# Split attention tiles: scores from scaled float16 pieces of q and k instead of fp32r pieces

## The chip, the cores and the metric

The kernel runs on one NeuronCore of one Trainium2 chip. The metric is the device time of one execution in microseconds (us); three executions of the kernel before gave 1159.14, 1161.74 and 1163.35, median 1161.74. The profile is of one execution.

Engines: TensorE (PE, with its weight loads shown as PEld), VectorE (DVE), ScalarE (ACT), GpSimd (POOL) and the queue that issues the DMAs (SP).

## The reference

```python
def _attn_ref(q, k, v, tau):                     # q, k, v: (8, 8, 576, 64) float32
    scale = 1.0 / np.sqrt(q.shape[-1])
    scores = scale * np.matmul(q, k.transpose(0, 1, 3, 2))
    thresh = np.max(scores, axis=-1, keepdims=True) - tau
    scores = np.where(scores >= thresh, scores, -1000000000.0)
    scores = scores - np.max(scores, axis=-1, keepdims=True)
    attn = np.exp(scores)
    attn = attn / (np.sum(attn, axis=-1, keepdims=True) + 1e-09)
    return np.matmul(attn, v).astype(np.float32)

def _moe_ref(x, w_in, w_out, s, b):              # x: (4608, 512), d_ff 2048
    r = np.maximum(x @ w_in, 0.0)
    return ((s * (r * r) + b) @ w_out).astype(np.float32)
```

The attention output, with its heads side by side, is the x of the second function.

## The kernel before

Batch 0 is computed by 36 "plain" tiles in full fp32. Batches 1 to 7 are computed by visits: a visit is one pair of heads of one batch, 28 in all, and has nine split tiles of 128 queries (four of head A, four of head B, and one shared tile of the 64 queries that are left in each head), 252 in all. "Split" means that a float32 matrix is written as a high and a low piece, and a product is made from matmuls of pieces.

One split tile runs as follows (`split_tile`). PE makes 128x576 scores in one of two PSUM tiles, s or t (L525): four matmuls of 288 columns, or six for the shared tile. DVE takes the negated row maximum (L528, `top`). POOL makes the threshold from it (L530, `line`), ACT the exponential with `top` as its bias (L532), DVE applies the threshold and sums (L534), POOL and DVE make the divisor (L537, L539), ACT and DVE write the two float16 pieces of the weights (L540, L542, L543), and SP issues a DMA transpose of them into ea or eb (L548). With the transposed pieces PE makes the product with v (`with_v`, L558, 28 matmuls for a group of 256 or 320 queries).

Before its tiles, a visit is prepared. `Head.load` reads k and q of both heads twice, once into each half of the 128 partitions of rk and rq (four DMAs of 288 KB). `Head.prepare` makes, for each head, a high piece of k on ACT (L377) and a low piece on POOL (L378), scales q by 1/8 on POOL (L384), makes q's high piece on ACT (L387) and its low piece on POOL (L388), and the pieces of the 64 queries left over (L391, L392). All these pieces are fp32r, 4 bytes each. For the shared tile two SP copies per head (L381) move the pieces of k to the tiles ow6 and kt1. khi, klo and qs exist once for head A and once for head B. `Values.prepare` finds the largest |v| of the visit: a DVE maximum (L418), a matmul with ones that sums it over partitions (L420), three small DVE operations (L421, L423, L426), and a POOL operation that scales v (L429).

The FFN runs on blocks of 256 rows in 16 steps of f: `step` has 12 matmuls of 256 columns (L769, h), a relu, a square and a float16 copy on ACT (L773, L776, L777), a low piece on POOL (L778), and two groups of three matmuls of 512 columns (L784, o). There are 288 steps. They fill PE around the attention.

The order on each engine is static. Every operation is given to `Plan.add` with an engine, a cost (how long it occupies the engine, and when its result is there), the buffers that it reads and writes, and a wished time; `Plan.run` places all of them by a list schedule forward and backward, and emits them in order of planned start. Each engine executes its own list in that order and waits for the results that it needs.

```python
        SMALLEST, SPREAD, E_SPREAD = 2.0 ** -60, 2.0 ** 13, 2.0 ** 15
        pe((4, 6)[len(ti.heads) - 1], HS, scores, ti.kq(), [bk], i - SCORES_AHEAD)
```

## Time and profile before

| | |
|---|---|
| three executions | 1159.14, 1161.74, 1163.35 us |
| profiled execution, first to last instruction (span) | 1157.2 us |
| median less span | 4.5 us |
| PE busy | 1132.1 us, 98% of the span, 8844 matmul records |
| ACT busy | 930.5 us, 80% |
| DVE busy | 855.2 us, 74% |
| POOL busy | 780.9 us, 67% |
| DMA queue of SP | 162.9 MB, 70% of 16 engines' span |

The profile lists no time of its own for the profiled execution beside its span. Busy times are unions of intervals on an engine. Matmuls are pipelined and their ends are modelled, so PE's rows are best read by the distance from one start to the next. The DMA queue's own waits are not counted as busy.

### The profile page before, as it was taken

Reading aid. Unit: us, or ns where it says so; the run is one execution under the profiler, and the core shown is the slowest. Engines: PE = TensorE matmul, PEld = TensorE weight load, DVE = VectorE, ACT = ScalarE, POOL = GpSimd, SP = SyncE. Lnnn points to the kernel's source line nnn. Section 1 sums busy time; section 2 is a strip of 40 time slices with the busy share of each in tenths; the row PEclk is TensorE's granted clock in tenths of the full one; section 3 lists DMA queues with packets and bytes.
Section 4 is the critical chain, followed back from the end, with each engine's and each line's share of the span. In section 5 each row is a group of like instructions: output and inputs, shape, how many; then the busy total and the mean of one; then the engine's idle time right before and its main releaser. Section 6 shows DMA issues by size and latency. Waiting matters only on the chain.

```text
span 1157.2 us, 26174 instructions
## 1 busy us (share of the span) xinstructions
PE 1132.1 (98%) x8844; PEld 828.1 (72%) x8844; DVE 855.2 (74%) x1782; ACT 930.5 (80%) x2161; POOL 780.9 (67%) x1326
## 2 busy tenths in 40 slices
...
GB/s 265 343 140 22 47 142 165 178 188 181 155 177 169 165 165 164 170 162 154 164 148 164 133 137 166 170 131 180 159 165 128 160 158 176 119 20 1 20 19 19
DMA packets 361334, 164.52 MB, mean 142 GB/s; under 512 B 315120, under 2 KB 336112, under 8 KB 361200
## 3 DMA queue, kind: packets, MB, share of 16 engines
...
## 4 chain that ended last, share of the span: by engine, by line
PE 83%; DMA 5%; ACT 4%; DVE 3%; issue 2%; SPq 1%; POOL 1%; DVEq 0%; ACTq 0%; POOLq 0%
PE o L784 30%; PE h L769 30%; PE pv L558 8%; PE s L525 6%; PE t L525 6%; DMA eb<-en 2%; DMA ea<-in_q_dram 1%; ACT em L475 1%; PE pv L504 1%; DMA rk<-in_k_dram 1%; DMA iw<-in_moe_w_in_dram 1%; PE s L468 1%; PE h L698 1%; PE t L491 1%; DMA rq<-in_q_dram 1%
## 5 line engine op out<-in xcount | busy, mean ns | idle before, releaser
L769 PE MATMUL h<-xp,iw 128*128 128x256 f16 x3456 | 426.9, 273 | 3.5 <-ACT iw L773 3.4
L769 PEld LDWEIGHTS <-iw 128*128 128x128 f16 x3456 | 330.2, 98 | 87.7 <-issue 9.2
L784 PE MATMUL o<-ow,gh 128*128 128x512 f16 x1080 | 324.2, 382 | 0.7 <-DVE iw L798 0.7
L778 POOL TENSOR_TENSOR gl<-iw,gh 128x256 f16<-128x256 f32 x272 | 202.6, 746 | 118.1 <-ACT gh L777 95.7
L543 DVE SCALAR_TENSOR_TENSOR en<-em,st,en 128x576 f16<-128x576 f32 x252 | 241.4, 962 | 21.3 <-ACT en L540 20.6
L540 ACT ACTIVATE en<-em,st 128x576 f16<-128x576 f32 x252 | 192.8, 770 | 16.5 <-DVE st L539 13.5
L784 PE MATMUL o<-ow,gl 128*128 128x512 f16 x540 | 205.4, 380 | 0.0
L773 ACT ACTIVATE iw<-h 128x256 f32<-128x256 f32 x288 | 109.3, 380 | 111.4 <-PE h L769 100.7
L784 PEld LDWEIGHTS <-gh 128*128 128x128 f16 x1152 | 101.7, 99 | 76.6 <-issue 5.0
L530 POOL TENSOR_SCALAR st<-st,bound 128x1 f32<-128x1 f32 x252 | 108.7, 432 | 52.8 <-DVE st L528 25.9
L776 ACT ACTIVATE iw<-iw 128x256 f32<-128x256 f32 x288 | 119.5, 415 | 3.9
L777 ACT CAST gh<-iw 128x256 f16<-128x256 f32 x288 | 115.8, 402 | 5.4 <-PE o L784 1.6
L534 DVE SCALAR_TENSOR_TENSOR em<-t,st,em 128x576 f32<-128x576 f32 x126 | 102.3, 812 | 24.1 <-ACT em L532 13.5
L537 POOL TENSOR_SCALAR st<-st 128x1 f32<-128x1 f32 x252 | 79.2, 314 | 58.0 <-DVE em L534 30.1
L534 DVE SCALAR_TENSOR_TENSOR em<-s,st,em 128x576 f32<-128x576 f32 x126 | 102.2, 811 | 21.4 <-POOL st L530 10.0
L528 DVE TENSOR_REDUCE st<-t 128x1 f32<-128x576 f32 x126 | 94.7, 751 | 26.4 <-PE t L525 25.4
L532 ACT ACTIVATE em<-s,st 128x576 f32<-128x576 f32 x126 | 92.7, 736 | 23.9 <-DVE st L528 23.1
L528 DVE TENSOR_REDUCE st<-s 128x1 f32<-128x576 f32 x126 | 94.6, 751 | 21.3 <-PE s L525 18.6
L558 PE MATMUL pv<-eb,v 128*64 128x256 f16 (+1 forms) x784 | 106.4, 288 | 2.8 <-DMA eb<-en 2.1
L558 PE MATMUL pv<-ea,v 128*64 128x256 f16 (+1 forms) x784 | 107.5, 288 | 0.0
L532 ACT ACTIVATE em<-t,st 128x576 f32<-128x576 f32 x126 | 92.6, 735 | 16.7 <-DVE st L528 15.8
L784 PEld LDWEIGHTS <-gl 128*128 128x128 f16 x576 | 56.5, 98 | 68.8 <-POOL gl L778 1.1
(190 smaller groups left out, 1873.8 us busy)
## 6 DMA issues: line engine op xcount, KB each, us to landing
...
ow<-k SPq DMA_DIRECT2D x56, 216.0 KB, 3.0
...
kt<-k SPq DMA_DIRECT2D x56, 72.0 KB, 2.8
```

The lines of the kernel that those rows point to most:

```text
L525: nc.tensor.matmul(ps[:, hf], stat, kk(hf), start=(n == 0), stop=(n == len(seq) - 1))
L528: dve((667, 750), lambda: nc.vector.tensor_reduce(out=top, in_=ps, axis=mybir.AxisListType.XY, op=ALU.max, negate=True), [bk], [(ks_, 0)], ...
L532: act((636, 740), lambda: nc.scalar.activation(out=halves, in_=ps, func=AF.Exp, bias=top, scale=1.0), [bk, (ks_, 0)], [em_k], i - 0.5)
L534: dve((740, 900), lambda: nc.vector.scalar_tensor_tensor(out=halves, in0=ps, scalar=line, in1=halves, op0=ALU.is_ge, op1=ALU.mult, accum_o ...
L540: act((668, 774), lambda: nc.scalar.activation(out=pieces[:, 0:S], in_=ex, func=AF.Copy, scale=unit), [em_k, (ks_, 3)], [en_k], i)
L543: dve2((740, 825), lambda: nc.vector.scalar_tensor_tensor(out=pieces[:, S + T:2 * S + T], in0=ex, scalar=unit, in1=pieces[:, 0:S], op0=ALU ...
L558: nc.tensor.matmul(ps[j * D:(j + 1) * D], hd.v[:, (n + 1) % 5, u * D:(u + 1) * D], lazy[("ea", "eb")[j]][:, n, g.c0:g.c0 + g.n], start=(i ...
L769: nc.tensor.matmul(ps, wi[w][f][:, c * P:(c + 1) * P], x[:, u, c, :], start=(c == 0 and i == 0), stop=(c == NC - 1 and i == 2))
L776: act((320, 417), lambda: nc.scalar.activation(out=g(), in_=g(), func=AF.Square), [kg], [kg], at)
L777: act((308, 405), lambda: nc.scalar.copy(out=hi, in_=g()), [kg], [f"gh{k3}"], at)
L778: do((712, 735) if not self.last else (340, 425), lambda: eng.tensor_tensor(out=lo, in0=g(), in1=hi, op=ALU.subtract), [kg, f"gh{k3}"], [f ...
L784: nc.tensor.matmul(bank["o"][:, t, :], a[:, ts_], w, start=(f == 0 and i == 0), stop=(f == NF - 1 and i == 2))
```

## The change

For the 28 visits (`class Visit` takes the place of `Values` and of the loads and preparations of `Head`):

- k and q are loaded once, two heads on 128 partitions, two DMAs of 288 KB per visit, into rk[:, n] and rq[:, n] with n the visit's number modulo 2.
- Maxima of |k|, |q| and |v| are taken (three DVE reductions), summed over partitions by one bf16 matmul, and turned into powers of two. POOL scales k and q by them (the factor of q holds the 1/8), ACT makes their high pieces in float16 and POOL their low pieces, on both heads at once. The pieces are kept for two visits.
- For each head, SP copies stack the pieces: both 64-partition halves of `y` get the two pieces of k (2 copies of 64x1152 float16), the upper half the high piece of q and the lower half the low one (2 copies of 64x512). That is 8 copies per visit in place of 4. The four stacks live in the tiles ow6 to ow9; the weights that stood there move into the first half of iw6 to iw9.
- A tile's scores are the same number of matmuls of the same columns, from float16 operands. The shared tile uses the pieces themselves and a small tile qt16.
- Scores are now larger by a power of two. POOL's threshold takes a per-visit limit (wz column 2), ACT makes the bias by a 128x1 operation of its own (L557 of the changed kernel), and the exponential takes the scale from wz column 1.
- The matmuls that sum norms over partitions take bf16 ones and bf16 squares instead of fp32. The planner's price for a matmul becomes 0.417 ns a column plus 3 ns.

```diff
-    qt, kt1 = const("qt", [P, 2, P], F32R), const("kt1", [P, HS], F32R)
+    qt = const("qt", [P, 2, P], F32R)
...
-    vm = const("vm", [P, 2], F32R)
+    vm = [const(f"vm{i}", [P, 4], BF16) for i in range(2)]
...
-            lazy["k"] = sb("k", [P, 4, S], F32R)
+            lazy["k"] = sb("k", [P, 8, S], F16)
...
-        def q(j):
-            lazy["qs", j] = sb(f"qs{j}", [P, M], F32R)
-        for j in range(2):
-            claim([f"q{j}"], lambda j=j: q(j))
-        def kp():
-            lazy["kp"] = sb(f"ow{PAIRS_IN}", [P, 2 * DM], F32R)
-        claim(["kp", (f"w{PAIRS_IN}", "o")] + [("kp", j, c) for j in range(2) for c in (0, S + HS)], kp)
-        claim(["k", "khi0", "klo0", "khi1", "klo1"], k)
+        claim(["k"] + [("piece", n, c) for n in range(2) for c in range(4)], k)
+        for n in range(2):
+            for j in range(2):
+                def y(n=n, j=j):
+                    lazy["y", n, j] = sb(f"ow{STACKS_IN + 2 * n + j}", [P, 4 * DM], F16)
+                claim([f"y{n}{j}", (f"w{STACKS_IN + 2 * n + j}", "o")] + [("y", n, j, c) for c in range(4)], y)
...
-        plan.add("PE", (n * (0.44 * cols + 6.5), n * (0.44 * cols + 6.5) + 170), fn, r, w, at)
+        plan.add("PE", (n * (0.417 * cols + 3), n * (0.417 * cols + 3) + 170), fn, r, w, at)
...
+            self.n, self.wz, self.kwz = i % 2, wz[i % 3], f"wz{i % 3}"
+            self.kpc = [("piece", self.n, c) for c in range(4)]
+            self.kqt = [(f"qt16_{self.n}", j) for j in range(2)]
+
+        def piece(self, c):
+
+            return lazy["k"][:, 4 * self.n + c]
+
+        def keys_of(self, j, u):
+
+            return lazy["y", self.n, j][:, u * S:(u + 1) * S]
+
+        def queries_of(self, j):
+
+            return lazy["y", self.n, j][:, 2 * S:2 * S + M]
...
+            for key, buf, ap in ("rk", rk, kT), ("rq", rq, qT):
+                load(288, lambda buf=buf, ap=ap: nc.sync.dma_start(out=buf[:, n], in_=ap[bi, h2].rearrange("h d s -> (h d) s")),
+                     [], [(key, n)], at)
...
+            raw = [(rk[:, n], ("rk", n)), (rq[:, n], ("rq", n))]
             flat = rv.rearrange("p h t d -> p (h t d)")
-            top = bank["pv"][:, 510:512]
-            dve((730, 819), lambda: nc.vector.tensor_reduce(
-                out=vm[:, 0:1], in_=flat, axis=mybir.AxisListType.X, op=ALU.max, apply_absolute_value=True), kr, ["vm"], at)
-            pe(1, 64, lambda: nc.tensor.matmul(top, ones, vm, start=True, stop=True), ["vm", "ones"], ["pv"], at)
+            ks = []
+            for c, (t, keys) in enumerate([(t, [k]) for t, k in raw] + [(flat, kr)]):
+                w = t.shape[-1]
+                ks.append((f"vm{n}", c))
+                dve((67 + 1.04 * w, 150 + 1.04 * w), lambda c=c, t=t: nc.vector.tensor_reduce(
+                    out=vm[n][:, c:c + 1], in_=t, axis=mybir.AxisListType.X, op=ALU.max, apply_absolute_value=True),
+                    keys, [ks[-1]], at)
+            top = bank["pv"][:, 500 + 4 * n:504 + 4 * n]
+            ktop = ("top", 500 + 4 * n)
+            pe(1, 64, lambda: nc.tensor.matmul(top, onesb, vm[n], start=True, stop=True), ks + ["onesb"], [ktop], at)
             dve((72, 155), lambda: nc.vector.tensor_scalar(
-                out=x[:, 0:1], in0=top[:, 0:1], scalar1=SMALLEST, scalar2=None, op0=ALU.max), ["pv"], [kx], at)
+                out=x[:, 0:3], in0=top[:, 0:3], scalar1=SMALLEST, scalar2=None, op0=ALU.max), [ktop], [kx], at)
             dve((72, 155), lambda: nc.vector.tensor_scalar(
-                out=x.bitcast(I32)[:, 1:2], in0=x.bitcast(I32)[:, 0:1], scalar1=EXPONENT, scalar2=EXPONENT,
+                out=x.bitcast(I32)[:, 3:6], in0=x.bitcast(I32)[:, 0:3], scalar1=EXPONENT, scalar2=EXPONENT,
                 op0=ALU.bitwise_and, op1=ALU.bitwise_xor), [kx], [(kx, 1)], at)
             dve((72, 155), lambda: nc.vector.tensor_scalar(
-                out=x.bitcast(I32)[:, 2:3], in0=x.bitcast(I32)[:, 0:1], scalar1=EXPONENT, scalar2=None,
+                out=x.bitcast(I32)[:, 6:9], in0=x.bitcast(I32)[:, 0:3], scalar1=EXPONENT, scalar2=None,
                 op0=ALU.bitwise_and), [kx], [(kx, 2)], at)
+            pool((270, 192), lambda: nc.gpsimd.tensor_tensor(
+                out=x[:, 9:12], in0=x[:, 3:6], in1=spread[:, 0:3], op=ALU.mult), [(kx, 1), "spread"], [(kx, 3)], at)
+
+            for c, (t, key) in enumerate(raw):
+                up = x[:, 9 + c:10 + c]
+                pool((722, 742), lambda t=t, up=up: nc.gpsimd.tensor_scalar(
+                    out=t, in0=t, scalar1=up, scalar2=1.0, op0=ALU.mult, op1=ALU.mult), [key, (kx, 3)], [key], at)
+                act((612, 717), lambda c=c, t=t: nc.scalar.copy(out=self.piece(2 * c), in_=t), [key], [self.kpc[2 * c]], at)
+                pool((1385, 1420), lambda c=c, t=t: nc.gpsimd.tensor_tensor(
+                    out=self.piece(2 * c + 1), in0=t, in1=self.piece(2 * c), op=ALU.subtract),
+                    [key, self.kpc[2 * c]], [self.kpc[2 * c + 1]], at)
+            for j in range(2):
+                own = slice(j * D, (j + 1) * D)
+                for u in range(2):
+                    to = slice(u * D, (u + 1) * D)
+                    dma(144, lambda j=j, own=own, to=to: nc.sync.dma_start(
+                        out=lazy["y", n, j][to, 0:2 * S].rearrange("p (u s) -> p u s", u=2), in_=lazy["k"][own, 4 * n:4 * n + 2]),
+                        self.kpc[0:2], [("y", n, j, u)], at)
+            for j in range(2):
+                own = slice(j * D, (j + 1) * D)
+                for u in range(2):
+                    to = slice(u * D, (u + 1) * D)
+                    dma(64, lambda j=j, own=own, to=to, u=u: nc.sync.dma_start(
+                        out=self.queries_of(j)[to], in_=self.piece(2 + u)[own, 0:M]), [self.kpc[2 + u]], [("y", n, j, 2 + u)], at)
+                pool((330, 330), lambda j=j, own=own: nc.gpsimd.tensor_copy(
+                    out=qt16[n][own, :, j * T:(j + 1) * T], in_=lazy["k"][own, 4 * n + 2:4 * n + 4, M:S]),
+                    self.kpc[2:4] + ["qt16"], [self.kqt[j]], at)
+            pool((270, 192), lambda: nc.gpsimd.tensor_scalar(
+                out=self.wz[:, 1:2], in0=x[:, 6:7], scalar1=0.25 / SPREAD ** 2, scalar2=x[:, 7:8], op0=ALU.mult, op1=ALU.mult),
+                [(kx, 2)], [(self.kwz, 1)], at)
+            pool((270, 192), lambda: nc.gpsimd.tensor_scalar(
+                out=self.wz[:, 2:3], in0=x[:, 3:4], scalar1=spread[:, 3:4], scalar2=x[:, 4:5], op0=ALU.mult, op1=ALU.mult),
+                [(kx, 1), "spread"], [(self.kwz, 2)], at)
...
-                seq = ti.st()
+                c, j = slice(hf * HS, (hf + 1) * HS), ti.slot
+                if j is None:
+                    seq = [(qt16[va.n][:, u], va.piece(w)[:, c]) for u, w in ((0, 0), (0, 1), (1, 0))]
+                else:
+                    seq = [(va.queries_of(j)[:, ti.n * P:(ti.n + 1) * P], va.keys_of(j, w)[:, c]) for w in range(2)]
                 for n, (stat, kk) in enumerate(seq):
-                    nc.tensor.matmul(ps[:, hf], stat, kk(hf), start=(n == 0), stop=(n == len(seq) - 1))
-        pe((4, 6)[len(ti.heads) - 1], HS, scores, ti.kq(), [bk], i - SCORES_AHEAD)
+                    nc.tensor.matmul(ps[:, hf], stat, kk, start=(n == 0), stop=(n == len(seq) - 1))
+        pe(6 if ti.slot is None else 4, HS, scores, va.kpc[0:2] + va.kqt if ti.slot is None else [("y", va.n, ti.slot, c) for c in range(4)],
+           [bk], i - SCORES_AHEAD)
 
         dve((667, 750), lambda: nc.vector.tensor_reduce(
             out=top, in_=ps, axis=mybir.AxisListType.XY, op=ALU.max, negate=True), [bk], [(ks_, 0)], i - SCORES_AHEAD)
         pool((260, 263), lambda: nc.gpsimd.tensor_scalar(
-            out=line, in0=top, scalar1=-1.0, scalar2=line_, op0=ALU.mult, op1=ALU.add), [(ks_, 0), "bound"], [(ks_, 1)], i - 0.5)
-        act((636, 740), lambda: nc.scalar.activation(out=halves, in_=ps, func=AF.Exp, bias=top, scale=1.0),
-            [bk, (ks_, 0)], [em_k], i - 0.5)
+            out=line, in0=top, scalar1=-1.0, scalar2=va.wz[:, 2:3], op0=ALU.mult, op1=ALU.add), [(ks_, 0), (va.kwz, 2)], [(ks_, 1)], i - 0.5)
+        act((100, 200), lambda: nc.scalar.activation(out=bias, in_=top, func=AF.Copy, scale=va.wz[:, 1:2]),
+            [(ks_, 0), (va.kwz, 1)], [(ks_, 4)], i - 0.5)
+        act((636, 740), lambda: nc.scalar.activation(out=halves, in_=ps, func=AF.Exp, bias=bias, scale=va.wz[:, 1:2]),
+            [bk, (ks_, 4), (va.kwz, 1)], [em_k], i - 0.5)
...
-        pe(1, 64, lambda: nc.tensor.matmul(bank["pv"][:, col:col + m], ones.bitcast(F32), nm[:, 0:m], start=True, stop=True),
-           ["ones", knm] + [(knm, u) for u in range(n)], [ktop], at)
+        pe(1, 64, lambda: nc.tensor.matmul(bank["pv"][:, col:col + m], onesb, nm[:, 0:m], start=True, stop=True),
+           ["onesb", knm] + [(knm, u) for u in range(n)], [ktop], at)
```

Three places in the order of instructions show it.

GpSimd, middle of the program, before: the preparation of one pair of heads stands one step at a time between the small operations of tiles (L530, L537) and the FFN (L778).

```order
L388 TENSOR_TENSOR qs_1047<-rq,qs_1047 64x512
L530 TENSOR_SCALAR st_74<-st_74,bound 128x1
L778 TENSOR_TENSOR gl_109<-iw_223,gh_106 128x256
L378 TENSOR_TENSOR k<-rk,k 128x576
L537 TENSOR_SCALAR st_74<-st_74 128x1
L530 TENSOR_SCALAR st_75<-st_75,bound 128x1
L388 TENSOR_TENSOR qs_1048<-rq,qs_1048 64x512
```

GpSimd, middle of the program, of the change: L415 makes the visit's factors, L420 scales k and q, L423 makes the low pieces; L555 and L564 are the tiles' small operations, L807 the FFN's.

```order
L415 TENSOR_TENSOR vs_104<-vs_104,spread 128x3
L420 TENSOR_SCALAR rk<-rk,vs_104 128x576
L420 TENSOR_SCALAR rq<-rq,vs_104 128x576
L423 TENSOR_TENSOR k<-rk,k 128x576
L423 TENSOR_TENSOR k<-rq,k 128x576
L555 TENSOR_SCALAR st_70<-st_70,wz_91 128x1
L442 TENSOR_SCALAR wz_92<-vs_104 128x1
```

The four long operations of a visit moved together, behind one small operation that needs the sum made by PE.

ScalarE, middle of the program, before: an exponential (L532) waits for DVE alone.

```order
L532 ACTIVATE em_80<-t,st_71 128x576 [waits DVE_49]
L773 ACTIVATE iw_443<-h 128x256 [waits PE_49]
L391 CAST qt<-rq 64x64
L776 ACTIVATE iw_443<-iw_443 128x256 [waits Activation_49]
L777 CAST gh_108<-iw_443 128x256 [waits Activation_49]
```

ScalarE, middle of the program, of the change: L557 is the small operation for the bias, L559 the exponential.

```order
L557 ACTIVATE st_72<-st_72,wz_90 128x1 [waits DVE_49]
L559 ACTIVATE em_78<-t,st_72,wz_90 128x576 [waits PE_49,Activation_49]
L567 ACTIVATE en_77<-em_80,st_71 128x576 [waits DMAHW5_49,DVE_49]
L569 COPY en_77<-en_77 128x64 [waits Activation_49]
L557 ACTIVATE st_73<-st_73,wz_90 128x1 [waits DVE_49]
```

The wait for DVE moved to the small operation, and the exponential waits for it.

TensorE, of the change, between the sum of maxima of the fifth of the 28 visits and that visit's first scores: L406 is the matmul that sums the maxima, L813 the FFN's, L585 products with v, L708 a sum of norms, L549 scores (each row repeated as often as the prediction says).

```order
L406 MATMUL pv<-vm_82,onesb 128x4
...
L813 MATMUL o<-ow_891,gh_115 128x512
...
L549 MATMUL t<-ow_1548 128x288
...
L585 MATMUL pv<-ea,v_106 64x256
...
L708 MATMUL pv<-nsq_86,onesb 128x2
...
L549 MATMUL s<-ow_1397 128x288
```

Before, the matmul that sums the maximum of v (L420) stood behind the first scores of its visit in all 28 visits; now it stands ahead of them, and the scores need what follows from it.

## Rows read from the trace of the kernel before

**Rows 1.** Busy time by stretch: us, then us (instructions) of each engine, clock, DMA share, GB/s

```profile
40.00:135.00 95.00, 89.41 (x794) 68.61 (x793) 86.66 (x172) 88.67 (x172) 69.38 (x112) 1.00 0.41 126
135.00:270.00 135.00, 126.75 (x967) 91.00 (x966) 118.72 (x254) 113.64 (x264) 103.23 (x171) 0.97 0.83 162
270.00:1030.00 760.00, 756.34 (x5986) 555.80 (x5984) 608.48 (x1269) 638.79 (x1522) 566.13 (x958) 1.00 0.82 154
1030.00:1157.00 127.00, 121.85 (x831) 80.95 (x828) 14.05 (x26) 56.31 (x139) 21.34 (x34) 1.00 0.06 18
```

**Rows 2.** Longest waits of PE, 135 to 270 us: total, times, longest

```profile
PE s L525 <- DVE em L534: 5.7, 3, 3.1
```

**Rows 3.** Timeline of PE, 500 to 512 us: start, duration, what, how many

```profile
503.19 1.47 PE L769 MATMUL h<-xp,iw 128*128 128x256 f16 x12
504.50 0.59 PE L784 MATMUL o<-ow,gh 128*128 128x512 f16 x2
...
507.09 1.47 PE L769 MATMUL h<-xp,iw 128*128 128x256 f16 x12
508.32 0.77 PE L525 MATMUL t<-k,qs 128*128 128x288 f32 x4
508.94 0.61 PE L784 MATMUL o<-ow,gh 128*128 128x512 f16 x2
```

**Rows 4.** Groups of matmuls by form: count, busy us, mean ns, idle before

```profile
L525 PE MATMUL s<-k,qs 128*128 128x288 f32 x448 | 92.6, 328 | 5.9 <-DVE em L534 5.7
...
L525 PE MATMUL s<-ow,qt 128*128 128x288 f32 x70 | 15.2, 322 | 0.0
...
L525 PE MATMUL s<-kt,qt 128*128 128x288 f32 x14 | 4.1, 294 | 0.0
...
L679 PE MATMUL pv<-norm,ones 128*128 128x2 f32 x32 | 4.6, 214 | 0.2 <-ACT en L540 0.2
```

**Rows 5.** Chain that ended last, 200 to 210 us: start, us, what

```profile
204.65 2.02 PE pv L558 x28
```

**Rows 6.** Timeline, 671.4 to 673.2 us: a sum of maxima and what follows

```profile
671.61 0.25 PE L420 MATMUL pv<-vm,ones 128*128 128x2 f32 x1
...
672.37 1.82 POOL L429 TENSOR_SCALAR rv<-rv,vs 128x640 f32<-128x640 f32 x1 [0.22 <-DVE vs L426]
```

**Rows 7.** Timeline, 835.4 to 838.6 us: the same in another visit

```profile
835.50 0.35 PE L420 MATMUL pv<-vm,ones 128*128 128x2 f32 x1
...
838.26 0.79 POOL L429 TENSOR_SCALAR rv<-rv,vs 128x640 f32<-128x640 f32 x1
```

**Rows 8.** Groups of GpSimd by form

```profile
L378 POOL TENSOR_TENSOR k<-rk,k 128x576 fp32r<-128x576 f32 x56 | 83.0, 1483 | 9.0 <-ACT k L377 3.3 <-DMA ea<-en 2.8 <-PE pv L420 1.2
...
L388 POOL TENSOR_TENSOR qs<-rq,qs 64x512 fp32r<-64x512 f32 x56 | 74.1, 1323 | 4.8 <-ACT en L542 0.3
L384 POOL TENSOR_SCALAR rq<-rq,bound 128x576 f32<-128x576 f32 x56 | 46.7, 836 | 28.5 <-DMA rq<-in_q_dram 24.5 <-PE pv L420 2.1 <-issue 0.3
...
L432 POOL TENSOR_SCALAR vs<-vs 128x1 f32<-128x1 f32 x28 | 8.8, 316 | 2.4
```

**Rows 9.** DMA issues: count, KB each, median us from issue to landing

```profile
ow<-k SPq DMA_DIRECT2D x56, 216.0 KB, 3.0
...
kt<-k SPq DMA_DIRECT2D x56, 72.0 KB, 2.8
```

**Rows 10.** Groups of ScalarE by form

```profile
L542 ACT COPY en<-en 128x64 f16<-128x64 f16 x252 | 59.4, 239 | 0.8
L377 ACT CAST k<-rk 128x576 fp32r<-128x576 f32 x56 | 37.3, 666 | 7.2 <-PE t L525 4.5 <-PE h L769 1.0 <-issue 0.8
L387 ACT CAST qs<-rq 128x512 fp32r<-128x512 f32 x56 | 34.7, 619 | 2.2 <-POOL rq L384 1.6 <-PE s L525 0.3 <-issue 0.2
```

**Rows 11.** Group of VectorE by form

```profile
L528 DVE TENSOR_REDUCE st<-s 128x1 f32<-128x576 f32 x126 | 94.6, 751 | 21.3 <-PE s L525 18.6 <-PE pv L420 1.3
```

**Rows 12.** Timeline of PE, 128 to 136 us: the first scores of a split tile

```profile
135.05 0.77 PE L525 MATMUL s<-k,qs 128*128 128x288 f32 x4
```

129 lines of the change are left out of this document (50 added, 79 removed).

## The prediction

> **What bounds the kernel now.** I read busy time by stretch first. From 270 to 1030 us PE is busy 756.3 of 760 us at full clock, while ACT is busy 84% (638.8), DVE 80% and POOL 74% [rows 1]. So there PE's own work sets the time, and the other engines have 120 to 190 us to spare. From 135 to 270 us, the first visits, PE lacks 8.3 us and the clock's mean is 0.97, which is about 4 us more at full clock; the longest waits there are scores that wait for a PSUM tile [rows 1, 2]. The end, 1030 to 1157 us, is FFN alone: 648 of its first matmuls stand behind the last scores, before and after, so the change does not touch it. From 40 to 135 us ACT is busy 88.7 of 95 us, DVE 86.7 and PE 89.4: there no engine has much to spare.
>
> So I price the change by what it takes from PE's own work, and by the waits that it adds to PE.
>
> **The scores themselves.** The price of one fp32r matmul of 288 columns comes from starts on PE's timeline. Twelve h matmuls take 504.50 - 503.19 = 1.31 us, 109 ns each; twelve o matmuls 507.09 - 504.50 = 2.59 us, 216 ns each. Twelve h and four scores take 508.94 - 507.09 = 1.85 us, so four scores take 0.54 us, 135 ns each [rows 3]. In float16 I put 288 columns on the line through 256 columns (109) and 512 (216): 122.5 ns. There are 448 + 70 + 14 score matmuls on s [rows 4] and, by the order, as many on t: 1064. The saving is 12.5 ns x 1064 = 13 us; since starts are given to 10 ns, four scores lie between 0.52 and 0.56 us, and the saving between 8 and 19 us. I take 12.
>
> **Sums over partitions.** The 18 sums of norms are fp32, seen as two records each; all of them together are busy 4.6 us [rows 4]. As one bf16 pass they lose about half: -2 us, between 0 and -4.6. The sum of maxima stays one short matmul per visit.
>
> **The other engines.** POOL loses 56 subtractions of 1.48, 56 of 1.32 and 56 scalings of 0.84 us (203.8 us together) and gets 56 subtractions and 56 scalings of the first and last kind (129.7) and 84 small operations of 0.32 (26.5) [rows 8]: 48 us less; the short operations on the 64 queries left over stay about as many. DVE gets 56 more maxima over 576 columns, 0.75 us each [rows 11]: +42 us, which in the long stretch brings it from 80% to about 85%. ACT loses 56 casts of 0.67 and 56 of 0.62 us (72 us), gets 56 of 0.67 back (37), and 252 bias operations that the trace has no row for. The nearest is the 128x64 copy, 0.24 us [rows 10]; with one column it can't cost more, nor less than nothing: 0 to 60 us. ACT changes by -35 to +25 us over the 895 us of the split phase, and stays below 90%. None of the three becomes the bound. In a tile's own chain the bias operation adds at most 0.24 us between the maximum and the exponential; a score tile is held in one of two PSUM tiles while PE does nearly 7 us of other work (760 us for about 220 tiles is 3.4 us a tile), so that is covered. The copies move 832 KB a visit instead of 576, but the loads 576 instead of 1152: SP issues two DMAs more per visit and carries less.
>
> **The wait that the change adds.** This is the term that decides. Before, k's and q's pieces needed no sum, and the sum of v's maximum stood behind a visit's first scores. Now the sum stands ahead of them, and from it to the first scores runs one chain: three small DVE operations, POOL's factors, two scalings and two subtractions, and the copy of q's low piece by SP. Its price:
> - from the sum to POOL's first operation 0.76 us in a clean case [rows 6] and 2.76 us where DVE was taken [rows 7]; I take the middle, 1.8;
> - on POOL 0.32 + 2 x 0.84 + 2 x 1.48 = 4.96 us [rows 8]; by the order 0 to 5 other operations stand between, 0.6 us of them on the mean: 5.5 (5.0 to 6.6);
> - the copy, 2.8 us from issue to landing for 72 KB and 3.0 for 216 KB [rows 9], so 2.8 for 64 KB;
> - two hand-overs, POOL to SP and DMA to PE, for which I put 0.4 together, a choice.
>
> That is 10.5 us, with 8.5 and 12.3 as bounds. What covers it is the PE work that the order places between the sum and the first scores. Counted with 109, 216 and 122.5 ns for the three forms, and 2.02 us for 28 products with v [rows 5], it is 5.2 us at the fifth visit (12 o, 4 scores, 28 products), 7.8 at the third, 9.0 at the first, 9.6 to 15 elsewhere, and 11.2 in the middle. Where the cover is short, PE waits for the rest. At 10.5 us the 28 visits lack 13.1 us together, 9.5 of it in the first five; at 8.5 us they lack 4.0, at 12.3 us 39.5 (16.3 in the first five).
>
> A rule of the Trainium skill speaks to the copy's price: "DMA: Bandwidth & Descriptors", Anatomy of one DMA, fits a fixed 2.0 us and 436 GB/s, for GpSimd's path. By it a 64 KB copy would take 2.2 us, the chain 9.9, the lack 8.5 us and the time about 5 us less than mine. The trace agrees that size hardly matters (72 and 216 KB differ by 0.2 us), but not on the fixed part, and I keep the measured 2.8.
>
> The first five visits lie in the stretch where the kernel before already loses 8.3 + 4 = 12.3 us. Their loads and buffers are loosened: k and q come in two DMAs and every piece has two visits' room, so I take the old loss as replaced, by 9.5 us of new waits and some 2 us of clock: net -1. The later visits add 3.6 us.
>
> **The start.** Up to the first split scores (135.05 us before [rows 12]) PE's lists are nearly the same: 108 h, all 72 plain scores, 175 against 180 transposes, 36 against 30 o. But the first relu of the FFN is the 180th row of ACT instead of the 156th. ACT's mean from 40 to 135 us is 88.67 / 172 = 0.52 us an instruction [rows 1], so 24 rows are 12 us; most of it is plain tiles that PE also does earlier, with 25 more transposes and 30 more products ahead of the first h. I take +2.5 us, between 0 and +6.
>
> **The sum.** 1157.2 - 12 - 2 - 1 + 3.6 + 2.5 = 1148.3 us of span. The median of the runs is 4.5 us above the profiled span; with the same distance the forecast is **1153 us**, 0.8% faster.
>
> **Rivals.**
> - *The visits run free* (chance 0.20). The order lets sums, pieces and copies run early, and the chain keeps within its cover. For it: POOL loses 48 us, each buffer has two copies, and this kernel's old chain through POOL rarely held PE after 270 us. Against it: the cover in the order is what the planner thought just enough, and it counts a 64 KB copy at 1.8 us, not 2.8. Then the early loss of 12.3 goes but for some 2 us, and 1157.2 - 12 - 2 - 10 + 0 = 1133, or 1138 us with the 4.5. The shorter copy of the page named above points this way.
> - *Nothing is left over* (0.17). The float16 scores gain only the lower 8 us, the sums of norms nothing, and the start costs the full 6: 1157.2 - 8 - 1 + 3.6 + 6 = 1157.8, or 1162 us.
> - *The chain is longer than its cover in most visits* (0.18, slower). Place: first scores of each visit, PE waiting for the copies into y. At 12.3 us the first five lack 16.3 + 2 against 12.3, the others 23.2: 1157.2 - 14 + 6 + 23.2 + 2.5 = 1175, or 1179 us. It decides from a chain of about 11.2 us on, where the lack eats the 14 us that PE saves. For it: the chain has nine steps on four in-order engines, and DVE and POOL are the two that were late in [rows 7]; a long wait can also halve the clock for a while, as happened twice before 270 us. Against it: the planner's list puts the five POOL steps close together.
>
> That fp32r weight loads set the pace of the scores, so that float16 would save far more, is excluded: a matmul with its load takes 135 ns in all [rows 3], 12 to 13 ns above the float16 line.
>
> **Chances and range.** Forecast 0.45 (1147 to 1158 us), the rivals as given. I count 0.3% (3.5 us) as what a measurement of this kernel can tell from no change. Nearly all of the forecast and all of the first rival are faster by more: 0.63. The second rival and the edges of its neighbours are within: 0.19. The third is slower: 0.18. For 8 in 10 the range leaves out the far half of the free case (below 1142) and of the slow one (above 1168).
>
> **What would show it.** In the profile after, a tile's four score matmuls take 0.49 us from start to start instead of 0.54; the sums of norms are single records; PE from 270 to 1030 us still has under 10 us of idle time. PE's waits ahead of the score line name a DMA into ow6 to ow9 (or POOL), some 13 us in total, the longest at the third and fifth visits. ACT's bias operations take 0.1 to 0.24 us. The first split scores begin at 135 to 141 us. The prediction is wrong if these waits exceed 25 us or the clock falls again and again, or if PE's waits move to the products with v because the eight copies hold back SP's transposes; and, on the other side, if the first visits run without waits.

## The result, and the profile after

The changed kernel takes 1172.04 us (median of four executions, 1171.52 to 1179.10) where the kernel before took 1160.44 on the same chip: a ratio of 1.0121, 95% interval 1.0088 to 1.0154. It is 1.2% slower. The forecast was 0.8% faster, and the time lies above the forecast's range. The profiled execution took 1172.21 us with a span of 1170.4. The experiments ran on several chips; each ratio is to the kernel before on the same chip, where its median lay between 1159.0 and 1160.4. One execution of the experiment e13, the profiled one, took 1451.68 us at a mean granted clock of 0.75; its ratio leaves it out, and no time is read from its profile.

The first view is busy time by stretch, with the columns of [rows 1]; the last four lines are extra stretches around 270 us.

```profile
40.00:135.00 95.00, 81.92 (x750) 63.01 (x747) 84.33 (x177) 87.22 (x165) 52.09 (x91) 0.98 0.42 141
135.00:270.00 135.00, 116.99 (x895) 78.32 (x893) 115.11 (x240) 112.21 (x268) 93.73 (x176) 0.96 0.72 144
270.00:1030.00 760.00, 747.29 (x5998) 519.64 (x5997) 630.10 (x1320) 673.12 (x1657) 525.13 (x982) 1.00 0.74 147
...
257.00:271.00 14.00, 6.00 (x37) 3.62 (x33) 11.40 (x22) 7.65 (x15) 9.21 (x20) 0.62 0.78 149
271.00:285.00 14.00, 14.00 (x112) 9.96 (x111) 12.32 (x25) 11.83 (x30) 5.47 (x11) 0.89 0.58 145
...
264.00:268.00 4.00, 2.02 (x8) 0.98 (x7) 3.08 (x4) 3.56 (x7) 2.24 (x8) 0.50 0.85 166
...
276.00:280.00 4.00, 4.00 (x32) 2.88 (x30) 3.60 (x7) 3.13 (x10) 1.83 (x6) 1.00 0.75 163
```

Against [rows 1], PE is busy 7.5 us less from 40 to 135 us, 9.8 less from 135 to 270 and 9.1 less after that. From 257 to 271 us it works only 6 of 14 us. While it stands there, the granted clock falls to half (1.2 GHz); within the next 14 us it is back at 2.4 GHz. PE's longest waits from 100 to 290 us (total, times, longest):

```profile
PE pv L708 <- DVE nsq L764: 5.0, 1, 5.0
PE h L798 <- ACT iw L802: 4.7, 5, 1.9
PE s L549 <- DMA ow<-k: 3.6, 3, 2.4
PE h L798 <- DVE xp L782: 2.3, 1, 2.3
```

The groups by form, to be held against [rows 4] and [rows 10], show that the operations themselves came out much as forecast on PE, and longer on ACT. The first line is of the kernel before, the others of the changed one:

```profile
L532 ACT ACTIVATE em<-s,st 128x576 f32<-128x576 f32 x126 | 92.7, 736 | 23.9 <-DVE st L528 23.1
...
L559 ACT ACTIVATE em<-s,st,wz 128x576 f32<-128x576 f32 x126 | 104.0, 825 | 1.2
...
L549 PE MATMUL s<-ow 128*128 128x288 f16 x448 | 74.3, 289 | 4.2 <-DMA ow<-k 4.0 <-DVE em L561 0.2
L549 PE MATMUL t<-ow 128*128 128x288 f16 x448 | 73.8, 288 | 1.4 <-DMA ow<-k 0.5 <-DVE em L561 0.4 <-issue 0.3
L557 ACT ACTIVATE st<-st,wz 128x1 f32<-128x1 f32 x252 | 72.6, 289 | 28.5 <-DVE st L553 25.7 <-DVE st L566 1.2 <-POOL rv L448 0.3
...
L708 PE MATMUL pv<-nsq,onesb 128*128 128x2 bf16 x16 | 2.7, 168 | 6.5 <-DVE nsq L764 6.5
```

**Where the start went.** The timeline has the first visit's preparation, and further down one tile's scores among FFN matmuls (start, us, what):

```profile
134.35 0.82 DVE L401 TENSOR_REDUCE vm<-rv 128x1 bf16<-128x640 f32 x1 [0.87 <-DMA rv<-in_v_dram]
...
135.55 0.17 PE L406 MATMUL pv<-vm,onesb 128*128 128x4 bf16 x1
...
137.93 0.19 POOL L415 TENSOR_TENSOR vs<-vs,spread 128x3 f32<-128x3 f32 x1
138.23 0.75 POOL L420 TENSOR_SCALAR rk<-rk,vs 128x576 f32<-128x576 f32 x1
...
141.76 1.72 POOL L423 TENSOR_TENSOR k<-rq,k 128x576 f16<-128x576 f32 x1
142.25 2.47 SPq L430 DMA_DIRECT2D ow<-k  x4
...
144.82 1.18 SPq L437 DMA_DIRECT2D ow<-k  x2
...
146.98 0.66 PE L549 MATMUL s<-ow 128*128 128x288 f16 x4 [0.62 <-DMA ow<-k]
...
502.32 1.47 PE L798 MATMUL h<-xp,iw 128*128 128x256 f16 x12
503.63 0.65 PE L549 MATMUL t<-ow 128*128 128x288 f16 x4
504.12 0.59 PE L813 MATMUL o<-ow,gh 128*128 128x512 f16 x2
```

The first split scores start at 146.98 us, against 135.05 before [rows 12]. From the sum of maxima (135.55) to them it is 11.4 us. But what does the sum wait for? It takes the maxima of k, q and v in one matmul, and v's came last, at 134.35 us. The two lines in question, L382 from 76 to 131 us and L401 from 70 to 148 us (durations in ns, shortest, median and longest, then first and last start; the maxima of k and q are those of the first two visits):

```profile
L382 SPq EVENT_SEMAPHORE  x1: 54370/54370/54370, 75.7 to 75.7; - x1
...
L401 DVE TENSOR_REDUCE vm<-rk x2: 746/748/750, 77.9 to 82.6; 128x1 bf16<-128x576 f32 x2
L401 DVE TENSOR_REDUCE vm<-rq x2: 747/748/748, 80.6 to 84.7; 128x1 bf16<-128x576 f32 x2
...
L401 DVE TENSOR_REDUCE vm<-rv x1: 824/824/824, 134.4 to 134.4; 128x1 bf16<-128x640 f32 x1
```

The first visit's maxima of k and q were there by 81.3 us. SP reached the load of v at 75.7 us and stood there for 54.4 us, because its buffer rv is also the second buffer of the plain tiles' transposed weights (`e32`: `(xb[2]..., rv...)[i % 2]`); in e5, which gives these another buffer, v's maximum is taken at 73.1 us. In the kernel before v had a sum of its own, and k and q waited for nothing of the kind. The same order of events is in every visit: in 27 of the 28 the sum starts 0.9 to 2.3 us after v's maximum (in one 6.9), the maxima of k and q lie 31 us or more before the sum, and the first scores come 10.1 to 16.9 us after it, median 11.7. v's load of one visit needs rv, which is free when the pieces of the v before are made, and these need a buffer that the products of the visit before hold (`vt[i % 3]`).

**The fifth visit.** Between a visit's sum and its first scores PE has only the work that the order put there. At the fifth visit this is the least:

```profile
250.70 0.18 PE L406 MATMUL pv<-vm,onesb 128*128 128x4 bf16 x1 [0.19 <-DVE vm L401]
...
256.05 0.30 PE L585 MATMUL pv<-eb,v 128*64 128x256 f16 x1 [1.62 <-DMA eb<-en]
...
262.78 0.19 PE L708 MATMUL pv<-nsq,onesb 128*128 128x2 bf16 x1 [5.01 <-DVE nsq L764]
263.54 1.14 PE L549 MATMUL s<-ow 128*128 128x288 f16 x4 [0.58 <-DMA ow<-k]
```

From the sum to the scores it is 12.8 us, and PE stands for 7.2 us of it. The profile puts most of this down to a transpose (eb<-en) and to the squares for a sum of norms (nsq). But the scores behind them then still wait for a copy into a stack, so without those two waits PE would have stood just as long, in front of the scores. The same holds at visits 1, 3, 8 and 21, whose first scores wait for a copy as well: in these five visits PE stands 1.9, 3.7, 7.2, 1.3 and 0.4 us between sum and first scores, 14.5 us in all.

**Lost time.** To compare kernels I gave each matmul record the pitch that it has in unbroken runs (109 ns for 256 columns, 216 for 512, 122.5 for 288 in float16 and 133 in fp32r, and so on), summed them to each instant, and took the rest of the time, from PE's first matmuls on, as lost to waits, to the clock and to changes of form. PE's work so counted is 1086.2 us before and 1074.5 after, 11.7 less. The lost time is 66.6 and 91.5, 24.9 more; together that is the 13.2 us of span. This table (us lost in each stretch of the profiled execution) has the kernels of the experiments too:

```
kernel                                      0-147  147-250  250-400  400-end   sum
before                                       24.4    13.7      8.1     20.4   66.6
after                                        35.6     8.9     22.7     24.3   91.5
e1  v's own sum                              28.4    10.8     12.2     14.7   66.1
e2  weights early                            30.8    15.7     23.8     24.0   94.3
e3  plain exponential                        34.3    11.2     20.9     20.0   86.4
e4  before, first visit behind v             23.3    15.0      9.9     21.1   69.3
e5  rv free of the plain tiles               36.8    13.3      6.3     20.7   77.1
e6  before, other order                      27.2    12.3     15.9     27.5   82.9
e7  v's own sum in the first visit           32.8    13.7     18.4     24.8   89.7
e8  e1, other exponential cost, 16 rounds    29.8     9.0     12.8     15.8   67.4
e9  one sum, v's buffers free                29.3     9.3     13.2     23.3   75.1
e10 fourth v buffer only                     32.8    11.0     19.9     20.8   84.5
e11 e1, other order                          27.9    13.3     15.1     18.9   75.2
e12 e9, 40 rounds                            28.7     9.0      8.3     16.7   62.7
e14 before, 40 rounds                        22.4    13.3      6.1     19.3   61.1
e15 e1 and e9 together, 40 rounds            29.9     7.3      6.5     16.5   60.2
e16 e12, plain exponential                   30.2     7.9      8.0     12.3   58.4
```

### The profile page after: what moved, and what is told of

Its sections match the earlier page's. It is cut to its first block, busy times and chain, and to the rows that moved or that the text cites. A ratio compares the mean times of both kernels' runs of the same rounds, so it can differ in the third digit from the quotient of the medians.

```text
span 1170.4 us, 26444 instructions
## 1 busy us (share of the span) xinstructions
PE 1117.2 (95%) x8826; PEld 781.3 (67%) x8826; DVE 874.8 (75%) x1838; ACT 965.8 (83%) x2301; POOL 721.4 (62%) x1369
## 4 chain that ended last, share of the span: by engine, by line
PE 61%; ACT 12%; DVE 8%; DMA 7%; issue 5%; POOL 4%; SPq 3%; DVEq 0%; POOLq 0%; ACTq 0%
PE h L798 23%; PE o L813 22%; PE pv L585 7%; PE s L549 4%; PE t L549 4%; ACT em L559 2%; ACT en L567 2%; DMA eb<-en 2%; DVE em L561 2%; DVE st L553 2%; DMA rv<-in_v_dram 1%; DMA ea<-in_q_dram 1%; DVE en L570 1%; POOL k L423 1%; ACT iw L802 1%
## 5 line engine op out<-in xcount | busy, mean ns | idle before, releaser
L807 POOL TENSOR_TENSOR gl<-iw,gh 128x256 f16<-128x256 f32 x272 | 195.9, 722 | 153.6 <-ACT gh L806 123.8
L813 PE MATMUL o<-ow,gh 128*128 128x512 f16 x864 | 256.9, 379 | 1.6 <-DVE iw L827 1.6
L570 DVE SCALAR_TENSOR_TENSOR en<-em,st,en 128x576 f16<-128x576 f32 x252 | 226.1, 901 | 24.1 <-ACT en L567 21.9
L813 PE MATMUL o<-ow,gl 128*128 128x512 f16 x432 | 163.7, 379 | 0.0
L555 POOL TENSOR_SCALAR st<-st,wz 128x1 f32<-128x1 f32 x252 | 121.5, 483 | 66.8 <-DVE st L553 48.3
L813 PEld LDWEIGHTS <-gh 128*128 128x128 f16 x1152 | 110.7, 98 | 77.7 <-issue 3.7
L564 POOL TENSOR_SCALAR st<-st 128x1 f32<-128x1 f32 x252 | 70.4, 279 | 81.6 <-DVE em L561 48.0
L549 PEld LDWEIGHTS <-ow 128*128 128x128 f16 x896 | 85.3, 98 | 48.4 <-issue 8.5
L561 DVE SCALAR_TENSOR_TENSOR em<-t,st,em 128x576 f32<-128x576 f32 x126 | 102.4, 813 | 14.4 <-ACT em L559 10.5
L585 PE MATMUL pv<-eb,v 128*64 128x256 f16 (+1 forms) x784 | 107.5, 289 | 5.2 <-DMA eb<-en 5.1
L585 PE MATMUL pv<-ea,v 128*64 128x256 f16 (+1 forms) x784 | 109.2, 290 | 1.3 <-DVE vs L407 1.3
L585 PEld LDWEIGHTS <-v 128*64 128x64 f16 x1568 | 85.0, 110 | 33.2 <-issue 17.7
L559 ACT ACTIVATE em<-s,st,wz 128x576 f32<-128x576 f32 x126 | 104.0, 825 | 1.2
L559 ACT ACTIVATE em<-t,st,wz 128x576 f32<-128x576 f32 x126 | 104.0, 826 | 1.0
```

Source lines behind the costliest of these rows:

```text
L549: nc.tensor.matmul(ps[:, hf], stat, kk, start=(n == 0), stop=(n == len(seq) - 1))
L555: pool((260, 263), lambda: nc.gpsimd.tensor_scalar(out=line, in0=top, scalar1=-1.0, scalar2=va.wz[:, 2:3], op0=ALU.mult, op1=ALU.add), [(k ...
L559: act((636, 740), lambda: nc.scalar.activation(out=halves, in_=ps, func=AF.Exp, bias=bias, scale=va.wz[:, 1:2]), [bk, (ks_, 4), (va.kwz, 1 ...
L561: dve((740, 900), lambda: nc.vector.scalar_tensor_tensor(out=halves, in0=ps, scalar=line, in1=halves, op0=ALU.is_ge, op1=ALU.mult, accum_o ...
L570: dve2((740, 825), lambda: nc.vector.scalar_tensor_tensor(out=pieces[:, S + T:2 * S + T], in0=ex, scalar=unit, in1=pieces[:, 0:S], op0=ALU ...
L585: nc.tensor.matmul(ps[j * D:(j + 1) * D], hd.v[:, (n + 1) % 5, u * D:(u + 1) * D], lazy[("ea", "eb")[j]][:, n, g.c0:g.c0 + g.n], start=(i ...
```

## The experiments

Theories: **V**, the one sum holds up k and q until v is there; **W**, the weights' loads come too late (first one issued at 22.0 us, 9.7 before); **A**, ScalarE's added work; **C**, the chain of operations from the sum to the first scores by itself, wherever the sum stands; **O**, the order that `Plan.run` happened to find.

**e1, a sum of its own for v.**

```diff
-            pe(1, 64, lambda: nc.tensor.matmul(top, onesb, vm[n], start=True, stop=True), ks + ["onesb"], [ktop], at)
...
+            def factors(c0, c1, ks, kx):
...
+                pe(1, 64, lambda: nc.tensor.matmul(top, onesb, vm[n][:, c0:c0 + 2], start=True, stop=True), ks + ["onesb"], [ktop], at)
...
+            factors(0, 2, [(f"vm{n}", c) for c in range(2)], kx)
...
+            kx = f"vsv{n}"
+            factors(2, 3, [(f"vm{n}", 2)], kx)
```

> The changed kernel, but the maxima of k and q go through one sum on TensorE and the maximum of v through a second one of its own (one more small matmul, three more small VectorE operations and one more of GpSimd in each visit). Theory V (the one sum for k, q and v puts k's and q's pieces behind the load of v, whose buffer the plain tiles hold until 131 us; the sum of maxima came at 135.5 us and the first split scores at 147.0): k's and q's maxima are summed well before 131 us, the first split scores start at 134 to 139 us, and the time falls by at least the 11 us lost at the start, to 1145 to 1160 us. Theory W (the loss is the late weights: the first weight load is issued at 22.0 us, not at 9.7, through the order that the planner settled on): unless that order moves too, 1168 to 1173 us. Theory A (ScalarE has too much work: 965.8 us busy, 35 more than before): no better than 1168 us, since ScalarE's work stays.

Measured: 1146.75 us, ratio to before 0.9896 (0.9872 to 0.9920). Its timeline has the first visit's sum of k and q and the first split scores:

```profile
84.90 0.18 PE L406 MATMUL pv<-vm,onesb 128*128 128x2 bf16 x1
...
134.82 0.65 PE L552 MATMUL s<-ow 128*128 128x288 f16 x4
...
149.81 0.81 DVE L399 TENSOR_REDUCE vm<-rv 128x1 bf16<-128x640 f32 x1
```

The sum is 50 us earlier, v's maximum comes after the first scores, and 25 us of the changed kernel's time are gone. W and A predicted no such thing. No visit's first scores wait for a copy any more.

**e2, the weights early.**

```diff
+START = [0, 2, 3, 1, 6, 8, 15, 16, 14, 7, 9, 19, 21, 25, 20, 26, 43, 27, 44, 45, 22, 46, 47, 30,
...
+        sp = [n for n, e in enumerate(engine) if e == "SP"]
+        for x, y in zip(START, START[1:]):
+            x, y = sp[x], sp[y]
+            before[y].append((x, occ[x]))
+            after[x].append((y, occ[y]))
```

> The changed kernel with the first 79 transfers of SyncE's queue (the loads of the plain pairs and of the weights) in the order of the kernel before; all else is left to the planner. Theory W: the weights are there as early as before, the first product with them starts at about 95 us, and the time falls by some 11 us, to about 1161 us. Theory V: the first split scores still wait for the load of v after 131 us and start at 145 to 149 us; the first product may come earlier, but the time stays within 1166 to 1175 us. Theory A: unchanged, 1172 us.

Measured: 1175.60 us (ratio 1.0139, 1.0116 to 1.0163). The first weights are loaded at 9.7 us again and the first product with them is 9.6 us earlier (101.1 us), yet nothing is gained; the first split scores are still late:

```profile
146.02 0.65 PE L555 MATMUL s<-ow 128*128 128x288 f16 x4
```

W falls: the late weights went with the late start and did not cause it.

**e3, the exponential as before, same order.**

```diff
-        act((100, 200), lambda: nc.scalar.activation(out=bias, in_=top, func=AF.Copy, scale=va.wz[:, 1:2]),
+        act((100, 200), lambda: None,
...
-        act((636, 740), lambda: nc.scalar.activation(out=halves, in_=ps, func=AF.Exp, bias=bias, scale=va.wz[:, 1:2]),
+        act((636, 740), lambda: nc.scalar.activation(out=halves, in_=ps, func=AF.Exp, bias=top, scale=1.0),
```

> The changed kernel in the same order of operations, with the small ScalarE operation for the bias left out and the exponential with the constant scale 1 and the negated maximum as bias, as before: it leaves out the un-scaling of the scores. Theory A: ScalarE loses 252 x (90 + about 60 to 100 ns) = 38 to 48 us of work and the tile's chain is some 0.2 us shorter, and most of the loss goes: 1160 us or less. Theories V and W: ScalarE's longer work lies beside TensorE's, the first split scores stay at 147 us, and the time stays at 1166 to 1173 us. The exponential itself should measure 736 ns again, not 825, if the scale operand is what made it longer.

Measured: 1167.15 us (ratio 1.0059, 1.0040 to 1.0077), 5 us below the changed kernel. Its group of exponentials:

```profile
L559 ACT ACTIVATE em<-s,st 128x576 f32<-128x576 f32 x126 | 92.5, 734 | 11.3 <-DVE st L553 8.2 <-DVE en L570 1.5 <-DVE st L566 0.9
```

The scale operand makes the exponential 91 ns longer. ScalarE's added work costs 5 us, so A is a part, and not the main one.

**e4, the kernel before with its first visit behind v.** The pieces of k and q of that visit read the key of v's factor.

```diff
+            after = [(f"vs{self.i // 2 % 2}", 1)] if first[self] < n_plain + 1 else []
...
-            act((565, 670), lambda: nc.scalar.copy(out=khi(), in_=k), pk, [f"khi{j}"], at)
+            act((565, 670), lambda: nc.scalar.copy(out=khi(), in_=k), pk + after, [f"khi{j}"], at)
...
```

> The kernel before, with the same operations, in which the order puts the pieces of k and q of the first split visit behind the scaling factor of v (for that one visit; nothing else is asked of the order). Theory V: the first split scores move from 135 us to 142 to 150 us and the time rises by 4 to 12 us, to 1164 to 1172 us. Theory W: no change of time unless the weights' loads come later too (first one issued at 9.7 us before). Theory A: no change, 1160 us.

Measured: 1163.20 us (ratio 1.0030, 1.0019 to 1.0041). The first split scores moved to 139.62 us, less than expected, the weights to 15.0 us, and the time rose by 3.5 us, just under what V expected. One visit behind v costs little; this run alone decides nothing.

**e5, rv free of the plain tiles** (one sum).

```diff
-        return (xb[2].rearrange("p c n -> p (c n)"), rv.rearrange("p h t d -> p (h t d)"))[i % 2][:, 0:5 * P].rearrange(
+        return (xb[2].rearrange("p c n -> p (c n)"), en[0])[i % 2][:, 0:5 * P].rearrange(
```

> The changed kernel with its one sum, but the second half of the plain tiles' transposes goes to another buffer (en0, 32 columns wider), so that rv is free from the start and the first visit's v can be loaded as early as its k and q; the second visit's v still has to wait until the pieces of the first one's v are made. Theory V: the sum of maxima of the first visit no longer waits for 131 us, and the first split scores start at 135 to 141 us; since the second visit's sum still waits for v, only a part comes back: 1158 to 1168 us. If the wait of the sum for v were of no account and only the operations of the chain counted (theory C: chain of 11.5 us from the sum to the first scores), the first scores would stay at 145 to 149 us and the time at 1169 to 1175 us.

Measured: 1158.17 us (ratio 0.9994, 0.9983 to 1.0004): 14 us back, by freeing a buffer. The first split scores start earlier than in any other kernel here:

```profile
122.46 0.65 PE L549 MATMUL s<-ow 128*128 128x288 f16 x4
```

But by 147 us this kernel has lost 36.8 us, more than the changed one; its gain lies after 250 us. So the time of the first scores is not by itself the measure of the loss at the start, and the first visit's wait for v is not what costs this kernel its time there. Its waits of PE from 80 to 400 us have one of 3.5 us for a plain tile's step on POOL:

```profile
PE t L510 <- POOL em L502: 5.0, 3, 3.5
```

That step stands in POOL's list behind the first visit's subtractions (L423, 105.5 to 108.7 us), so by this row an early preparation gets in the way of the plain tiles. The clock is at half twice before 147 us.

**e6, the kernel before in another order.**

```diff
-        for _ in range(4):
+        for _ in range(1):
```

> The kernel before with the same operations and dependencies, but with the order of the first of its rounds of ordering instead of the best of four: a plain measure of how much a worse order costs without any of the changed operations. Theory O (all of the loss is an unlucky order; the changed dependencies are of no account): as much slower as the changed kernel is, 1168 to 1175 us, with first split scores late as well. Theory V: some loss (0 to 10 us, 1160 to 1170 us), but the first split scores stay at 133 to 139 us, since k and q wait for no v here.

Measured: 1176.99 us (ratio 1.0155, 1.0130 to 1.0180). The same operations and dependencies are 18 us slower, and the first split scores are at 143.61 us, with no v to wait for. V's expectation missed here, O's by 2 us, and O has to be taken seriously: a difference of 10 us between two kernels with different orders proves no cause.

**e7, a sum of its own only in the first visit** (with the `factors` of e1).

```diff
+            own = self.i == min(values)
+            factors(0, 2 if own else 3, [(f"vm{n}", c) for c in range(2 if own else 3)], kx, [] if own else [f"vsv{n}"])
```

> The kernel with a sum of its own for v, but only in the first visit; the 27 others have one sum for k, q and v as in the changed kernel. It parts the loss in two: at the start (11 us more lost by 147 us than before) and later (14 us more lost after it). Theory V in its whole form (v's load holds up k and q in every visit, through the single buffer rv): the first split scores at 134 to 140 us, but the loss after 147 us stays for the most part, and the time is 1155 to 1165 us. If the start is all of it: 1145 to 1150 us, as with the sum of its own everywhere (1146.75 us).

Measured: 1171.01 us (ratio 1.0102, 1.0077 to 1.0125), no gain, although the first split scores start at 129.57 us. Both expectations missed. The loss after 147 us stays, as V has it, and most of the loss before it as well (32.8 us against 28.4 in e1). PE's longest wait there is for the relu of the first FFN step, 4.9 us up to 113.3 us:

```profile
PE h L805 <- ACT iw L809: 9.4, 5, 4.9
```

This relu stands in ACT's list behind scalings of the weights (L703), and the clock is at half for 10 us from 109 us on. That is a matter of the order and no wait for v.

**e8, e1 with another cost and 16 rounds.**

```diff
-        for _ in range(4):
+        for _ in range(16):
...
-        act((636, 740), lambda: nc.scalar.activation(out=halves, in_=ps, func=AF.Exp, bias=bias, scale=va.wz[:, 1:2]),
+        act((725, 829), lambda: nc.scalar.activation(out=halves, in_=ps, func=AF.Exp, bias=bias, scale=va.wz[:, 1:2]),
```

> The kernel with a sum of its own for v in every visit, whose order is made with a cost of the exponential nearer to the one measured (725 instead of 636 ns, for 825 measured against 736) and in 16 rounds instead of 4: no operation is changed. If the order still leaves something on TensorE, it is 2 to 6 us faster than the 1146.75 us of that kernel: 1140 to 1145 us. If what is left (66.1 us of TensorE not at work at its pitch, most of it before 135 us) is set by the start's own chain, it stays within 1144 to 1149 us.

Measured: 1148.99 us (ratio 0.9913, 0.9894 to 0.9932). Nothing more was to be had this way; a second order of the same kernel gives nearly the same time.

**e9 and e10, v's buffers free, with one sum.** e10 has a fourth buffer for v's pieces, in the space of the zeros that only the plain stage needs (the matmuls that keep PE busy at the very start read ones instead); e9 has that and the edit of e5.

```diff
-    vt = [const(f"v{i}", [P, 5, P], F16) for i in range(3)]
+    vt = [const(f"v{i}", [P, 5, P], F16) for i in range(3)] + [v3.bitcast(F16).rearrange("p (t d) -> p t d", t=5)]
...
-            self.v, self.kvs = vt[i % 3], [("v", i % 3)]
+            self.v, self.kvs = vt[(i + 2) % 4], [("v", (i + 2) % 4)]
```

> The changed kernel with its one sum for k, q and v and every operation of the chain, but v's buffers no longer hold it up: the plain tiles' transposes use en0 instead of rv, and there is a fourth buffer for the pieces of v (in the space of the zeros that only the plain stage needs), so that a visit's v pieces needn't wait for the products of the visit before, nor the next v's load for these pieces. Theory V (k and q wait for v through the one sum, in every visit): nearly all comes back as with a sum of its own, 1143 to 1153 us, and the sum comes well over 12 us ahead of the first scores in most visits. Theory C (the chain of 11.7 us from the sum to the first scores is what costs): no gain beyond the 14 us of the first buffer alone (1158.17 us), 1156 to 1162 us. Theory O (the order found is good or bad by chance): anything between 1145 and 1177 us.

> The changed kernel with the fourth buffer for the pieces of v alone; the first visit's v still waits for the plain tiles. Theory V: the loss of the start stays (first split scores at 143 to 149 us) and most of what is lost after 270 us comes back (30.9 us from 270 us to the end in the changed kernel, 18.5 with a sum of its own): 1157 to 1166 us. Theory O: anything between 1145 and 1177 us.

Measured: e10 1161.65 us (ratio 1.0024, 1.0008 to 1.0040), 10 us below the changed kernel; its first split scores stay at 146.72 us, both as V expected:

```profile
146.72 0.66 PE L551 MATMUL s<-ow 128*128 128x288 f16 x4 [0.89 <-DMA ow<-k]
```

Its sums now lie 19.1 us ahead of the first scores in the median, against 11.7 in the changed kernel. But the loss after 250 us, most of which should have come back, fell from 47.0 us to 40.7 only (26.9 in e1); the profiled execution is 3.5 us above the median.

e9 1156.88 us (ratio 0.9984, 0.9970 to 0.9999): 15 us below the changed kernel, but only 1.3 below e5, where V expected 1143 to 1153, and within what C expected. The other half of V's expectation held: the sums come 12.1 us or more ahead of the first scores (median 19.6), and no visit's first scores wait for a copy.

**e11, e1 in another order**, and **e12, e9 with 40 rounds**: the one line of `range` again, 1 and 40.

> The kernel with a sum of its own for v, with the order of the first round of ordering instead of the best of four: the same control as for the kernel before, where this cost 18 us. Theory O (the order alone makes the differences): some 10 to 20 us slower than 1146.75 us, 1157 to 1167 us, so that dependencies decide nothing that an order doesn't. Theory V (looser dependencies leave an order more room, and a poor one costs less): 1148 to 1156 us, still faster than every order of the kernel with one sum.

> The kernel of the first of these four (one sum, v's buffers free) with 40 rounds of ordering instead of 4; no operation changes. If the order still leaves TensorE time beside the start: 2 to 6 us less than with 4 rounds, 1139 to 1148 us; if not, the same within 2 us.

Measured: e11 1156.60 us (ratio 0.9978, 0.9966 to 0.9991), 10 us slower than e1 and between the two expectations, so a poor order costs here as well, if less than the 18 us of e6. e12 1144.90 us (ratio 0.9880, 0.9852 to 0.9908), 12 us faster than e9 with the same operations. The chain from the sum to the first scores is all there in e12, with its sums 13.5 us or more ahead of the first scores (median 19.6), and so C falls: the chain costs where the sum cannot come early, and what e9 lacked was order.

**e13, the changed kernel with 40 rounds**, and **e14, the kernel before with 40 rounds.**

> The changed kernel, operations and dependencies untouched, with 40 rounds of ordering instead of 4. Theory O (the order found was unlucky, the dependencies are of no account): near the 1144.9 us that 40 rounds gave with v's buffers free, 1143 to 1152 us. Theory V (k and q wait for v through the one sum, whatever the order): no order takes away that wait; the first split scores stay at 142 to 149 us, the sum stays some 12 us ahead of the first scores, and the time is 1160 to 1172 us.

> The kernel before, untouched but for 40 rounds of ordering instead of 4: what the kernel before would have been at the same effort. It gains 0 to 9 us, 1150 to 1159 us; the changed operations, with v's buffers free (1144.9 us at 40 rounds), should then still be some 5 to 14 us ahead of it, about the 12 us that the cheaper products were worked out to be worth.

Measured: e13 1172.45 us (ratio 1.0101, 1.0080 to 1.0122), in an order that differs from the changed kernel's on all four compute engines. e14 1153.23 us (ratio 0.9943, 0.9926 to 0.9960). Ten times the rounds gained nothing under the changed kernel's dependencies, and 27.5 us less time is reached at the same effort when v's buffers are free (e12). This is the run that speaks against O as the cause of the loss.

**e15, both remedies, 40 rounds**, and **e16, e12 with e3's edit.**

> A sum of its own for v and v's buffers free together, 40 rounds. Theory V: the two remove the same wait, so together they give no more than either alone with a good order: 1142 to 1147 us. If each removed a wait of its own, 1138 us or less.

> The kernel with one sum, v's buffers free and 40 rounds, in the same order of operations, with the bias operation left out and the exponential with the constant scale 1 and the negated maximum as bias: it leaves out the un-scaling of the scores, as e3 did in the changed kernel's order (5 us less there). Theory A in its weak form (ScalarE's extra work costs something only where the order leaves no room): 0 to 3 us less than 1144.9 us. If the extra ScalarE work costs the same everywhere: 5 us less, 1138 to 1141 us.

Measured: e15 1142.08 us (ratio 0.9850, 0.9835 to 0.9864), the fastest complete kernel here. Two remedies give 3 us more than one (e12) and 5 us more than the other (e1, at 4 rounds), as V expected if they remove the same wait. Its busy time by stretch, to hold against [rows 1]:

```profile
40.00:135.00 95.00, 84.69 (x774) 65.16 (x771) 86.97 (x188) 88.51 (x170) 72.89 (x124) 1.00 0.45 133
135.00:270.00 135.00, 129.98 (x1024) 88.27 (x1023) 124.63 (x285) 119.74 (x297) 102.31 (x193) 0.99 0.78 152
270.00:1030.00 760.00, 755.00 (x6079) 526.27 (x6077) 617.04 (x1358) 664.03 (x1650) 515.47 (x989) 1.00 0.73 143
```

e16 1138.42 us (ratio 0.9811, 0.9792 to 0.9830), 6.5 us less than e12: ScalarE's added work costs 5 to 6.5 us in a poor order and in a good one.

**e17 and e18, e15 with the bias made by VectorE or GpSimd.**

```diff
-        act((100, 200), lambda: nc.scalar.activation(out=bias, in_=top, func=AF.Copy, scale=va.wz[:, 1:2]),
+        dve((72, 155), lambda: nc.vector.tensor_scalar(out=bias, in0=top, scalar1=va.wz[:, 1:2], scalar2=None, op0=ALU.mult),
```

> The fastest complete kernel so far (a sum of its own for v, v's buffers free, 40 rounds; 1142.08 us) with the tile's bias made by VectorE, right behind the maximum that it is made from, instead of by ScalarE. If the bias operation is the larger part of the 5 to 6.5 us that ScalarE's added work was worth, 1136 to 1140 us; if the longer exponential is, or if VectorE's 252 added operations take as much away, 1141 to 1145 us.

> The same with the bias made by GpSimd: ScalarE is as free as with VectorE, but the exponential waits for a handover to GpSimd and back. If what counts is ScalarE's busy time, the same gain as on VectorE (1136 to 1140 us); if it is the length of the tile's chain, slower than 1142 us, 1143 to 1150 us.

Measured: 1152.23 us (ratio 0.9934, 0.9913 to 0.9955) and 1147.32 us (0.9885, 0.9869 to 0.9902), both slower than e15. e17 missed both of its expectations; e18 lies where the length of the tile's chain counts. The orders differ too (by 147 us e17 has lost 34.0 us, e15 29.9), so what the bias operation costs apart from the exponential stays open.

## Why the prediction was wrong

- **The scores (-12) and the sums of norms (-2): right, if a little large.** Twelve h and four scores take 504.12 - 502.32 = 1.80 us where they took 1.85 [rows 3], so a score matmul is 12.5 ns shorter there, and 10.5 by the pitches above. The 16 two-column sums of norms are busy 2.7 us instead of 4.6 [rows 4]. PE's counted work fell by 11.7 us.
- **The start (+2.5, 0 to 6): the step that failed.** It measured 35.6 - 24.4 = 11.2 us by 147 us. PE stands 18.5 us by then against 7.8 before, in waits of at most 1.8 us, most of them at plain tiles and FFN steps. The step compared lists ("PE's lists are nearly the same") and the distance of the first relu in ACT's rows. It did not ask what the first visit's sum waits for, though the code says it: the sum takes v's maximum, v lies in rv, and the plain tiles write rv. With k and q free of v in every visit the start loses 3.5 to 5.4 us more than before (e1, e8, e9, e11), and at 40 rounds 6.3 and 7.5 more than e14 (e12, e15). So the tie is a part of the 11.2 and not all. Freeing the first visit alone did not bring the loss down to that (12.4 more than before in e5, 8.4 in e7), so by which waits the tie costs time at the start stays open.
- **The wait that the change adds: the mechanism right, 14.5 us where 13.1 were forecast.** The chain was put at 10.5 us and measured 11.4 in the first visit and 11.7 in the median. In the first visit it took 2.4 us from the sum to POOL, 5.5 on POOL as forecast, and 2.0 for the copy with 1.3 before it behind other copies. By name PE waited for copies only 4.5 us in all. Counted as above, under whatever name, it is 14.5 us in visits 1, 3, 5, 8 and 21, with the fifth (7.2) and third (3.7) the longest, as forecast. The sum cannot move ahead of v, and so the order cannot put more work behind it: with v's buffers free it comes 19.6 us ahead in the median, and these waits are gone (e9, e12).
- **The first five visits (-1): mis-sized.** From 147 to 400 us, which takes in four later visits, the kernel lost 31.6 us against 21.8 before, 9.8 more. The new waits of visits 1, 3 and 5 are 12.8 us instead of 9.5; the clock, put at some 2 us, cost about 4 behind the fifth visit alone; and the old loss was not simply replaced: from 147 to 250 us only 4.8 us of it went.
- **The later visits (+3.6): about right in size.** From 400 us on the kernel lost 3.9 us more than before, but hardly any of it in front of a visit's first scores, and ACT's added work has a share in it (e3).
- **ACT: outside its bounds.** I put the bias operation at no more than the 0.24 us of a 64-column copy; it takes 289 ns, and the exponential's 89 ns (825 against 736) were not in the sum at all. ACT's busy time from 270 to 1030 us rose by 34.3 us, where the bound for the whole split phase was +25. It stayed below 90% (88.6), and still costs 5 to 6.5 us (e3, e16). The Trainium skill has this price: "ScalarE: Activation LUTs", What ACT_TABLE_LOAD costs, says that each one-column operand adds about 93 ns. The traces agree, with 89 and 91.
- **The copies: 2.2 us for 64 KB and 2.5 for 144**, not 2.8. The rule of the Trainium skill that I set against my price ("DMA: Bandwidth & Descriptors", Anatomy of one DMA) gives an estimate of 2.2 for 64 KB, and the trace agrees with it.
- **The slower rival** named what happened at the fifth visit, a chain longer than its cover and a clock that halves behind a long wait. But it had this in most visits, where it is five of 28, and it had the start at 2.5 us, so that its time near the one measured (1179) is luck.

What is shown: with k and q tied to v in every visit the operations take 1172.0, 1175.6 and 1172.5 us in three orders (after, e2, e13); with one of the two buffers freed 1158.2 and 1161.7 (e5, e10); with the tie gone 1142.1 to 1156.9 in six kernels and orders (e1, e8, e9, e11, e12, e15). In none of these six do a visit's first scores wait for a copy; in the changed kernel and in e2, e3, e5, e7 and e10 those of two to five visits do. At 40 rounds the changed operations beat the kernel before by 8.3 us (e12) to 11.1 us (e15, 1142.08 against 1153.23), close to the 11.7 us of work that they save. What is open: by which waits the tie costs time at the start, where e5 and e7 lose as much for reasons of their own; and how much of the 25 us between the changed kernel and e1 is the tie's own and how much a lucky order, which can make 10 us of it (e1 against e11).
